# Window attention with a Mish FFN: weight pieces taken apart in pairs, on VectorE and ACT alone

## The chip, the cores and the metric

The kernel runs on one core of a Trainium2 chip. The metric is the device time of one execution in microseconds (us); a kernel is measured by the median of several runs. In the profile PE is TensorE (PEld its weight loads), DVE is VectorE, ACT is ScalarE, POOL is GpSimd, and SP is the engine whose queue issues the DMAs.

## The reference, cut to what matters

```python
def _attn_ref(q, k, v):            # q, k, v: 8 x 8 x 576 x 64
    scores = np.matmul(q, k.transpose(0, 1, 3, 2)) / np.sqrt(D)
    scores = np.where((rel >= 0) & (rel < 64), scores, -1000000000.0)
    attn = np.exp(scores - np.max(scores, axis=-1, keepdims=True))
    attn = attn / (np.sum(attn, axis=-1, keepdims=True) + 1e-09)
    return np.matmul(attn, v)

def _moe_ref(x, w_in, w_out):      # x: 4608 x 512, w_in: 512 x 2048, w_out: 2048 x 512
    h = x @ w_in
    sp = np.where(h > 20.0, h, np.log1p(np.exp(np.minimum(h, 20.0))))
    return ((h * np.tanh(sp)) @ w_out)
```

The two weight matrices are float64. The rest is float32.

## The kernel before, in words

The 4608 tokens go through in twelve chunks of 384. A chunk has an attention part (four pairs of heads) and then an FFN part of sixteen steps, one for each block of 128 hidden features. One step's FFN-in is twelve matmuls of 384 columns into `h_ps` (line 195): every product is made of three, high by high, high by low and low by high, since activations and weights are both held as a rounded high part and a rest. VectorE takes the minimum `t` (line 202), ACT applies four functions (lines 203, 208, 209, 210), VectorE multiplies (line 212), and ACT or POOL makes the high part `gh` and POOL the rest `gl` (line 217). FFN-out is nine matmuls of 512 columns into three accumulators (line 230) and follows two steps behind. `h_ps` has two buffers.

The weights come as 64-bit words and are taken apart on the core, in the program's first part, while chunk 0's attention and its first FFN steps run. `load_w` (line 242) handles one piece of 512 columns: a DMA of 512 KB into `st` (three buffers, line 245), the absolute value on ACT (line 251), a clamp (line 252), three bit operations on VectorE (lines 254 to 256) that build the float32 value `wa`, a rounded copy on ACT (line 257: `wi_h` or `wo_h`) and a subtraction (line 258: `wi_l` or `wo_l`). For a piece of the first matrix POOL clamps and VectorE subtracts; for one of the second VectorE clamps and POOL subtracts. So there are 32 pieces, and VectorE has 128 weight operations of 512 columns: 32 of each of lines 254, 255 and 256, 16 of line 252 and 16 of line 258.

Seven pieces are asked for among chunk 0's attention and two at each of its FFN steps (`take_w`). Eight steps of chunk 0 run alone, then they alternate with chunk 1's. Within that the order of each engine's instructions is set by the framework's scheduler, not by the order of the source. All loads are issued by SP, in one queue.

The program's first two chunks and the third transpose the probabilities on PE and copy them to `pT`, one half on ACT and one on VectorE (line 172).

Of the kernel before, what the change touches and what calls it, by code (L numbers as in the profile page):

```python
# [20 lines left out]
BIG = float(np.array(0x47EFFFFF, np.uint32).view(np.float32))  # L21
WP = 512


@with_exitstack
def tile_window_attn_mish_ffn(
# [45 lines left out]
    for j in range(2):  # L72
        m = const.tile([P, P], F32, name=f"mask{j}")
# [4 lines left out]
    wi_h = const.tile([P, NF, NC_, P], F32R, name="wi_h")
    wi_l = const.tile([P, NF, NC_, P], F32R, name="wi_l")
    wo_h = const.tile([P, NF, DO], F32R, name="wo_h")  # L80
    wo_l = const.tile([P, NF, DO], F32R, name="wo_l")
# [72 lines left out]
    def att_transpose(c, p, pr):  # L154
        pT = next(pTs)
        if c > 2:


            tr = ap_.tile([P, P // 32, HM, 32], F32, name="tr", tag="pr", bufs=2)
            nc.vector.transpose(tr.rearrange("p k j i -> p j k i"),  # L160
                                pr.rearrange("p j (k i) -> p j k i", i=32))
            for r in range(0, P, 32):
                for k in range(0, P, 32):
                    if 0 <= k - r % BLK <= BLK:
                        nc.sync.dma_start(pT[k:k + 32, r // 32, :, :], tr[r:r + 32, k // 32, :, :])
            return pT
        for h in range(2):
            t_ps = (bank(c, p, "t_ps") if c else ps_h.tile([P, CH], F32, name="t_ps", tag="h_ps")
                    ).rearrange("p (m k) -> p m k", k=P)
            for m in range(NM):  # L170
                nc.tensor.transpose(t_ps[:, m, :], pr[:, h * NM + m, :], ident)  # L171
            (nc.scalar.copy if h == 0 else nc.vector.tensor_copy)(
                pT[:, :, h * NM:(h + 1) * NM, :].rearrange("p r m i -> p m r i"),
                t_ps.rearrange("p m (r i) -> p m r i", i=32))
        return pT
# [13 lines left out]
    def ffn_in(c, x, f, alone=False):  # L189
        xh, xl = x  # L190
        h_ps = ps_h.tile([P, CH], F32, name="h_ps", tag="h_ps")
        n = 0
        for cc in range(NC_):
            for w, xx in ((wi_h, xh), (wi_h, xl), (wi_l, xh)):
                nc.tensor.matmul(h_ps, w[:, f, cc, :], xx[:, cc, :], start=n == 0, stop=n == 3 * NC_ - 1)  # L195
# [64 lines left out]
    def load_w_in(f):  # L260
        load_w(w_in[f].rearrange("p c f -> p (c f)"), wi_h[:, f, :, :].rearrange("p c f -> p (c f)"),
               wi_l[:, f, :, :].rearrange("p c f -> p (c f)"), True)

    def load_w_out(f):
        load_w(w_out[f], wo_h[:, f, :], wo_l[:, f, :], False)


    class Att:
# [17 lines left out]
        def transpose(self, p):  # L286
            self.pT[p] = att_transpose(self.c, p, self.pr.pop(p))
# [36 lines left out]
    todo_w = [(load_w_in, 0)]  # L324
    for f in range(NF):
        todo_w += [(load_w_in, f + 1)] * (f + 1 < NF) + [(load_w_out, f)]

    def take_w(n):
        for _ in range(min(n, len(todo_w))):
            w, f = todo_w.pop(0)  # L330
            w(f)

# [83 lines left out]
```

## Time and profile before

| What | us |
|---|---|
| Median of 3 runs (993.81 to 995.67) | 994.03 |
| The profiled execution | 995.3 |
| Its span, first to last instruction | 993.5 |
| PE busy | 946.5 (95%) |
| VectorE busy | 491.8 (50%) |
| ACT busy | 631.4 (64%) |
| POOL busy | 328.8 (33%) |

The profile shows one execution. Busy shares are averages over the span: the first 120 us look different from the rest. Matmuls are pipelined, and a busy PE is not PE at its peak. The granted clock of TensorE has two levels, 1.2 and 2.4 GHz; 1.00 means 2.4 GHz throughout a stretch.

### The profile page before, as it was taken

Reading aid. Unit: us, or ns where it says so; the run is one execution under the profiler, and the core shown is the slowest. Engines: PE = TensorE matmul, PEld = TensorE weight load, DVE = VectorE, ACT = ScalarE, POOL = GpSimd, SP = SyncE. Lnnn points to the kernel's source line nnn. Section 1 sums busy time; section 2 is a strip of 40 time slices with the busy share of each in tenths; the row PEclk is TensorE's granted clock in tenths of the full one; section 3 lists DMA queues with packets and bytes.
Section 4 is the critical chain, followed back from the end, with each engine's and each line's share of the span. In section 5 each row is a group of like instructions: output and inputs, shape, how many; then the busy total and the mean of one; then the engine's idle time right before and its main releaser. Section 6 shows DMA issues by size and latency. Waiting matters only on the chain.

```text
span 993.5 us, 18088 instructions
## 1 busy us (share of the span) xinstructions
PE 946.5 (95%) x6408; PEld 821.4 (83%) x6408; DVE 491.8 (50%) x1352; ACT 631.4 (64%) x1525; POOL 328.8 (33%) x419
## 2 busy tenths in 40 slices
PE   4696699998999999999999999999999999999998
PEld 3585599886888888888888888888888888888996
DVE  6799874444444454444454453453443543543222
ACT  5667676664666666665665666666665665666664
POOL 2243463321333333323333323323333333333333
PEclk8787899997999999999999999999999999999999
DMA  7565420123221221331221221221231221310000
GB/s 240 188 194 161 143 85 1 49 68 111 66 69 54 89 69 42 88 83 42 88 83 43 89 81 45 86 83 46 84 80 47 85 74 43 97 39 13 32 1 32
DMA packets 82649, 77.34 MB, mean 78 GB/s; under 512 B 10368, under 2 KB 73856, under 8 KB 82560
## 3 DMA queue, kind: packets, MB, share of 16 engines
q1 hardware_dynamic: 82560, 76.19, 25.5%
q8 instruction: 51, 0.84, 0.4%
q14 instruction: 38, 0.31, 0.1%
HBM read 56.10 MB, written 9.44 MB: 66 GB/s over the span
## 4 chain that ended last, share of the span: by engine, by line
PE 87%; DVE 6%; DMA 2%; ACT 2%; issue 1%; SPq 0%; ACTq 0%; POOL 0%; DVEq 0%; POOLq 0%
PE h_ps L195 40%; PE acc L230 38%; PE s_ps L128 4%; PE o_ps L184 4%; DMA st<-w_out 2%; DVE wa L256 1%; DVE wa L255 1%; DMA st<-w_in 1%; ACT pr L141 1%; PE t_ps L171 1%; DVE wa L252 0%; DVE wi_l L258 0%; DVE wa L254 0%; DVE t L212 0%; ACT wa L251 0%
## 5 line engine op out<-in xcount | busy, mean ns | idle before, releaser
L195 PE MATMUL h_ps<-xh,wi_h 128*128 128x384 f32 x768 | 267.8, 349 | 13.6 <-DVE t L212 12.3
L216 POOL TENSOR_SCALAR gh<-t 128x384 fp32r<-128x384 f32 x176 | 90.7, 515 | 550.1 <-DVE t L212 504.0
L195 PE MATMUL h_ps<-xh,wi_l 128*128 128x384 f32 x768 | 263.7, 343 | 0.0
L195 PE MATMUL h_ps<-xl,wi_h 128*128 128x384 f32 x768 | 263.3, 343 | 0.0
L203 ACT ACTIVATE t<-t 128x384 f32<-128x384 f32 x192 | 100.5, 524 | 237.2 <-DVE t L202 237.2
L230 PE MATMUL acc<-wo_l,gh 128*128 128x512 f32 x576 | 227.0, 394 | 0.0
L230 PE MATMUL acc<-wo_h,gh 128*128 128x512 f32 x576 | 226.4, 393 | 0.5 <-POOL gh L216 0.5
L212 DVE SCALAR_TENSOR_TENSOR t<-t,h_ps 128x384 f32<-128x384 f32 x176 | 96.9, 550 | 250.3 <-ACT t L210 249.9
L217 POOL TENSOR_TENSOR gl<-t,gh 128x384 fp32r<-128x384 f32 x192 | 197.2, 1027 | 32.8 <-ACT gh L214 18.2
L230 PE MATMUL acc<-wo_h,gl 128*128 128x512 f32 x576 | 206.8, 394 | 0.0
L195 PEld LDWEIGHTS h_ps<-xh,wi_h 128*128 128x128 f32 x768 | 147.0, 192 | 28.5 <-DVE t L212 14.6
L195 PEld LDWEIGHTS h_ps<-xl,wi_h 128*128 128x128 f32 x768 | 147.4, 192 | 8.1 <-issue 1.9
L195 PEld LDWEIGHTS h_ps<-xh,wi_l 128*128 128x128 f32 x768 | 147.5, 192 | 1.1 <-issue 0.2
L202 DVE TENSOR_SCALAR t<-h_ps 128x384 f32<-128x384 f32 x192 | 106.6, 556 | 63.2 <-PE h_ps L195 55.8
L141 ACT ACTIVATE pr<-pr,mx 128x128 f32<-128x128 f32 x288 | 111.8, 390 | 38.0 <-DVE mx L138 38.0
L230 PEld LDWEIGHTS acc<-wo_h,gl 128*128 128x128 f32 x576 | 107.4, 188 | 23.7 <-issue 1.5
L230 PEld LDWEIGHTS acc<-wo_h,gh 128*128 128x128 f32 x576 | 109.1, 189 | 17.6 <-POOL gh L216 0.9
L230 PEld LDWEIGHTS acc<-wo_l,gh 128*128 128x128 f32 x576 | 108.9, 189 | 16.6
L209 ACT ACTIVATE t<-t,half_b 128x384 f32<-128x384 f32 x192 | 118.2, 616 | 5.4
L208 ACT ACTIVATE t<-t,one_b 128x384 f32<-128x384 f32 x192 | 118.1, 616 | 5.1
L210 ACT ACTIVATE t<-t 128x384 f32<-128x384 f32 x192 | 100.4, 524 | 5.6
L138 DVE CUSTOM_DVE_ANT_0 pr<-s_ps,mask 128x128 f32<-128x128 f32 x288 | 65.3, 286 | 60.7 <-PE s_ps L128 60.7
(49 smaller groups left out, 693.3 us busy)
## 6 DMA issues: line engine op xcount, KB each, us to landing
v_t<-vN SPq DMA_DIRECT2D x48, 384.0 KB, 3.6
k_t<-kT SPq DMA_DIRECT2D x47, 224.0 KB, 3.0
pT<-tr SPq DMA_DIRECT2D x432, 24.0 KB, 1.8
out<-o SPq DMA_DIRECT2D x36, 256.0 KB, 2.3
q_t<-qT SPq DMA_DIRECT2D x47, 192.0 KB, 2.5
st<-w_in SPq DMA_DIRECT2D x16, 512.0 KB, 4.4
st<-w_out SPq DMA_DIRECT2D x16, 512.0 KB, 3.4
q_t<-qT SPq DMA_DIRECT2D x3, 64.0 KB, 2.1
```

The costliest lines, as they stand in the source:

```text
L138: nc.vector.tensor_tensor_reduce(out=pr[:, j, :], in0=s_ps[h][:, m, :], in1=mk, op0=ALU.add, op1=ALU.min, scale=-0.125, scalar=3.0e38, acc ...
L141: nc.scalar.activation(pr[:, j, :], pr[:, j, :], AF.Exp, bias=mx[:, j:j + 1], scale=-1.0, accum_out=sm[:, j:j + 1])
L195: nc.tensor.matmul(h_ps, w[:, f, cc, :], xx[:, cc, :], start=n == 0, stop=n == 3 * NC_ - 1)
L202: nc.vector.tensor_scalar(t, h_ps, 20.0, None, ALU.min)
L203: nc.scalar.activation(t, t, AF.Exp)
L208: nc.scalar.activation(t, t, AF.Square, bias=one_b)
L209: nc.scalar.activation(t, t, AF.Ln, bias=half_b, scale=0.5)
L210: nc.scalar.activation(t, t, AF.Exp, scale=-1.0)
L212: nc.vector.scalar_tensor_tensor(t, t, -1.0, h, ALU.add, ALU.mult)
L216: nc.gpsimd.tensor_scalar(gh, t, 1.0, 0.0, ALU.mult, ALU.add)
L217: nc.gpsimd.tensor_tensor(gl, t, gh.bitcast(F32), ALU.subtract)
L230: nc.tensor.matmul(acc[t], a[:, ts_], w[:, f, :], start=f == 0 and i == 0, stop=f == NF - 1 and i == 2)
```

## The change

The host lays both pieces of a step side by side, 1024 columns, in one array `w`. `load_w` (now line 245) loads them with one DMA of 1 MB and takes them apart together: one ACT operation for the absolute value, five VectorE operations (clamp, line 258; three bit operations, 260 to 262; subtraction, 267), one rounded copy on ACT. POOL has no part in it. A piece is loaded into memory of its own, which later holds the step's high and low parts; from the fourth on, a load waits for the last bit operation of the third piece before it. VectorE has 80 weight operations of 1024 columns: 32 with one tensor as input (lines 258 and 260) and 48 with two. Four pieces are asked for among chunk 0's attention and one at each FFN step of chunk 0. Chunk 1's second half of `pT` is copied by ACT too.

```diff
-        st = mp.tile([P, WP], I64, name="st", bufs=3, tag="st")
-        nc.sync.dma_start(st, src)
+        st = const.tile([P, 2 * WP], I64, name="st", tag=f"w{f}")
+        dma = nc.sync.dma_start(st, w[f])
+        if f >= 3:
+            tc.add_manual_dep(dma.ins, used[f - 3].ins.name, SYNC, reason="pace")
...
-        a = mp.tile([P, WP], U32, name="wa", tag="t", bufs=4)
+        a = mp.tile([P, 2 * WP], U32, name="wa", bufs=2)
         af = a.bitcast(F32)
         nc.scalar.activation(af, hi.bitcast(F32), AF.Abs)
-        (nc.gpsimd if first else nc.vector).tensor_scalar(af, af, BIG, TINY, ALU.min, ALU.max)
+        nc.vector.tensor_scalar(af, af, BIG, TINY, ALU.min, ALU.max)
...
+        ws.append(const.tile([P, 2, 2, WP], F32R, name="w", tag=f"w{f}"))
+        wh, wl = ws[f][:, :, 0, :], ws[f][:, :, 1, :]
         nc.scalar.copy(wh, af)
-        (nc.vector if first else nc.gpsimd).tensor_tensor(wl, af, wh.bitcast(F32), ALU.subtract)
+        nc.vector.tensor_tensor(wl, af, wh.bitcast(F32), ALU.subtract)
...
-            (nc.scalar.copy if h == 0 else nc.vector.tensor_copy)(
+            (nc.scalar.copy if h == 0 or c == 1 else nc.vector.tensor_copy)(
...
-            take_w(2)
+            take_w()
```

The scheduler makes another order of it. On VectorE, this is the place of the tenth and eleventh step's `t` (the row with x2; line 202 before, 203 now), ahead of it and behind. Before:

```order
L252 TENSOR_SCALAR wa<-wa 128x512
L254 TENSOR_SCALAR wa<-wa 128x512 x2
L255 SCALAR_TENSOR_TENSOR wa<-st,wa 128x512 x2
L256 SCALAR_TENSOR_TENSOR wa<-st,wa 128x512 x2
L202 TENSOR_SCALAR t<-h_ps 128x384 x2
L258 TENSOR_TENSOR wi_l<-wa,wi_h 128x512
L252 TENSOR_SCALAR wa<-wa 128x512
L254 TENSOR_SCALAR wa<-wa 128x512 x2
L255 SCALAR_TENSOR_TENSOR wa<-st,wa 128x512
L212 SCALAR_TENSOR_TENSOR t<-t,h_ps 128x384
L255 SCALAR_TENSOR_TENSOR wa<-st,wa 128x512
L212 SCALAR_TENSOR_TENSOR t<-t,h_ps 128x384
```

The same place in the change:

```order
L267 TENSOR_TENSOR w<-wa,w 128x2x512
L261 SCALAR_TENSOR_TENSOR wa<-st,wa 128x1024
L262 SCALAR_TENSOR_TENSOR wa<-st,wa 128x1024
L187 TENSOR_TENSOR xl_577<-o_ps,xh_576 128x384
L267 TENSOR_TENSOR w<-wa,w 128x2x512
L203 TENSOR_SCALAR t<-h_ps 128x384 x2
L213 SCALAR_TENSOR_TENSOR t<-t,h_ps 128x384 x2
L203 TENSOR_SCALAR t<-h_ps 128x384
L213 SCALAR_TENSOR_TENSOR t<-t,h_ps 128x384
```

The first row with x2 of `t` has 99 of the 128 weight operations ahead of it before, and all 80 of the 80 in the change; nothing of the weights stands behind it.

On SP, the loads from the first weight piece on. Before:

```order
L245 DMA st<-w_in 128x512
L105 DMA q_t<-qT 128x384
L107 DMA k_t<-kT 128x448
L114 DMA v_t<-vN 128x6x128
L245 DMA st<-w_in 128x512
L114 DMA v_t<-vN 128x6x128
L105 DMA q_t<-qT 128x384
L107 DMA k_t<-kT 128x448
L245 DMA st<-w_out 128x512
```

The same place in the change:

```order
L248 DMA st<-w 128x1024
L105 DMA q_t<-qT 128x384
L107 DMA k_t<-kT 128x448
L114 DMA v_t<-vN 128x6x128 x2
L248 DMA st<-w 128x1024
L105 DMA q_t<-qT 128x384
L107 DMA k_t<-kT 128x448
L248 DMA st<-w 128x1024
```

The places of the weights' loads are nearly the same; each carries twice the bytes.

## Rows read from the trace of the kernel before

**Rows 1.** Windows: length, busy us of PE, PEld, DVE, ACT, POOL; PEclk, DMA, GB/s.

```profile
6.00:50.00 44.00, 26.64 (x272) 20.41 (x274) 36.50 (x133) 28.38 (x93) 8.21 (x8) 0.80 0.69 223
50.00:117.40 67.40, 57.54 (x355) 49.56 (x351) 64.64 (x134) 47.39 (x113) 29.82 (x25) 0.85 0.54 168
117.40:123.80 6.40, 0.11 (x1) 0.00 (x0) 4.38 (x10) 5.68 (x12) 1.89 (x2) 0.82 0.45 164
123.80:128.30 4.50, 4.48 (x14) 4.38 (x15) 3.81 (x6) 1.75 (x3) 4.29 (x4) 0.50 0.37 116
128.30:230.00 101.70, 101.70 (x641) 89.68 (x640) 51.18 (x129) 68.49 (x157) 36.27 (x42) 1.00 0.16 50
```

**Rows 2.** Chain of waits, 110 to 140 us: start, length, what.

```profile
115.04 1.29 DVE wa L255 x2
...
123.22 0.56 DVE t L212
...
123.82 4.21 PE h_ps L195 x12
...
134.43 2.08 PE h_ps L195 x12
```

**Rows 3.** Groups on VectorE, 0 to 117.40 us: busy, mean ns, idle ahead.

```profile
L256 DVE SCALAR_TENSOR_TENSOR wa<-st,wa 128x512 uint32<-128x512 uint32 x25 | 23.4, 939 | 0.0
L255 DVE SCALAR_TENSOR_TENSOR wa<-st,wa 128x512 uint32<-128x512 uint32 x25 | 19.6, 795 | 0.1
L254 DVE TENSOR_SCALAR wa<-wa 128x512 uint32<-128x512 uint32 x25 | 11.3, 464 | 0.4 <-POOL wa L252 0.2
L138 DVE CUSTOM_DVE_ANT_0 pr<-s_ps,mask 128x128 f32<-128x128 f32 x48 | 11.0, 283 | 9.4 <-PE s_ps L128 9.4
L258 DVE TENSOR_TENSOR wi_l<-wa,wi_h 128x512 fp32r<-128x512 f32 x12 | 10.3, 858 | 0.2 <-ACT wi_h L257 0.2
L252 DVE TENSOR_SCALAR wa<-wa 128x512 f32<-128x512 f32 x12 | 5.6, 464 | 3.7 <-ACT wa L251 3.6
L202 DVE TENSOR_SCALAR t<-h_ps 128x384 f32<-128x384 f32 x9 | 4.9, 548 | 0.7 <-PE h_ps L195 0.7
...
L172 DVE COPY pT<-t_ps 128x384 f32<-128x384 f32 x8 | 4.4, 545 | 0.0
...
L145 DVE TENSOR_SCALAR sm<-sm 128x3 f32<-128x3 f32 x8 | 1.5, 191 | 1.5 <-ACT pr L141 1.5
```

**Rows 4.** Groups on VectorE, 160 to 230 us: a 768-column operation.

```profile
L151 DVE TENSOR_TENSOR pr<-pr,sm 128x768 f32<-128x768 f32 x4 | 3.8, 954 | 0.1
```

**Rows 5.** Tile `wa`: shortest, median and longest duration in ns.

```profile
L254 DVE TENSOR_SCALAR wa<-wa x32: 410/420/1528, 10.4 to 151.1; 128x512 uint32<-128x512 uint32 x32
...
L256 DVE SCALAR_TENSOR_TENSOR wa<-st,wa x32: 674/686/1753, 12.7 to 153.1; 128x512 uint32<-128x512 uint32 x32
```

**Rows 6.** Timeline, POOL at 98 us, then VectorE: start, length, operation.

```profile
98.08 1.33 POOL L258 TENSOR_TENSOR wo_l<-wa,wo_h 128x512 fp32r<-128x512 f32 x1 [4.55 <-ACT wo_h L257]
...
54.92 0.95 DVE L252 TENSOR_SCALAR wa<-wa 128x512 f32<-128x512 f32 x1 [0.99 <-ACT wa L251]
...
98.21 1.75 DVE L256 SCALAR_TENSOR_TENSOR wa<-st,wa 128x512 uint32<-128x512 uint32 x1
...
112.67 1.32 DVE L258 TENSOR_TENSOR wi_l<-wa,wi_h 128x512 fp32r<-128x512 f32 x1 [0.22 <-ACT wi_h L257]
...
117.45 1.02 DVE L202 TENSOR_SCALAR t<-h_ps 128x384 f32<-128x384 f32 x2
```

**Rows 7.** Windows, 10 to 20 us, when the first loads land.

```profile
10.00:20.00 10.00, 5.60 (x69) 4.08 (x62) 9.02 (x39) 6.21 (x22) 1.12 (x2) 0.83 0.92 320
```

**Rows 8.** Waits of SP's DMA queue, 0 to 120 us: total, times, longest.

```profile
SPq L245 <- DVE wa L256: 78.2, 22, 7.4
```

**Rows 9.** Timeline of ACT at the restart, 116 to 131 us.

```profile
121.35 1.10 ACT L209 ACTIVATE t<-t,half_b 128x384 f32<-128x384 f32 x2
122.36 0.92 ACT L210 ACTIVATE t<-t 128x384 f32<-128x384 f32 x2
```

More of the change, by code (lines that the diff above doesn't have):

```diff
@@ L21 @@
 BIG = float(np.array(0x47EFFFFF, np.uint32).view(np.float32))
+SYNC = mybir.DependencyInfo(mybir.DependencyClass.Sync, mybir.DependencyReason.DATA)
 WP = 512
@@ L31, in tile_window_attn_mish_ffn @@
     vN: bass.AP,
-    w_in: bass.AP,
-    w_out: bass.AP,
+    w: bass.AP,
     out: bass.AP,
@@ L38, in tile_window_attn_mish_ffn @@
     NPAIR, _, NT = qT.shape
-    NF, _, NC_, _ = w_in.shape
-    DO = w_out.shape[2]
+    NF = w.shape[0]
+    DO = out.shape[1]
+    NC_ = NPAIR
     CH = 384
@@ L76, in tile_window_attn_mish_ffn @@
         firsts.append(m)
[L78 to L81, printed above, removed]
+    ws = []
     pTs = [const.tile([P, P // 32, HM, 32], F32, name=f"pT{i}") for i in range(2)]
@@ L193, in ffn_in @@
         for cc in range(NC_):
-            for w, xx in ((wi_h, xh), (wi_h, xl), (wi_l, xh)):
-                nc.tensor.matmul(h_ps, w[:, f, cc, :], xx[:, cc, :], start=n == 0, stop=n == 3 * NC_ - 1)
+            for part, xx in ((0, xh), (0, xl), (1, xh)):
+                nc.tensor.matmul(h_ps, ws[f][:, 0, part, cc * P:(cc + 1) * P], xx[:, cc, :],
+                                 start=n == 0, stop=n == 3 * NC_ - 1)
                 n += 1
@@ L228, in ffn_out @@
             ts_ = slice(t * P, (t + 1) * P)
-            for i, (a, w) in enumerate(((gh, wo_h), (gh, wo_l), (gl, wo_h))):
-                nc.tensor.matmul(acc[t], a[:, ts_], w[:, f, :],
+            for i, (a, part) in enumerate(((gh, 0), (gh, 1), (gl, 0))):
+                nc.tensor.matmul(acc[t], a[:, ts_], ws[f][:, 1, part, :],
                                  start=f == 0 and i == 0, stop=f == NF - 1 and i == 2)
@@ L234, in ffn_store @@
         for t in range(NTT):
-            o = mp.tile([P, DO], F32, name="o", bufs=3, tag="st")
+            o = mp.tile([P, DO], F32, name="o", bufs=3)
             if t % 2 == 0:
@@ L240, in ffn_store, with load_w @@
             nc.sync.dma_start(out[c * CH + t * P:c * CH + (t + 1) * P, :], o)
-    def load_w(src, wh, wl, first):
-        st = mp.tile([P, WP], I64, name="st", bufs=3, tag="st")
-        nc.sync.dma_start(st, src)
+    used = []
+    def load_w(f):
+        st = const.tile([P, 2 * WP], I64, name="st", tag=f"w{f}")
+        dma = nc.sync.dma_start(st, w[f])
+        if f >= 3:
+            tc.add_manual_dep(dma.ins, used[f - 3].ins.name, SYNC, reason="pace")
         words = st.bitcast(U32).rearrange("p (n two) -> p n two", two=2)
         lo, hi = words[:, :, 0], words[:, :, 1]
-        a = mp.tile([P, WP], U32, name="wa", tag="t", bufs=4)
+        a = mp.tile([P, 2 * WP], U32, name="wa", bufs=2)
         af = a.bitcast(F32)
         nc.scalar.activation(af, hi.bitcast(F32), AF.Abs)
-        (nc.gpsimd if first else nc.vector).tensor_scalar(af, af, BIG, TINY, ALU.min, ALU.max)
+        nc.vector.tensor_scalar(af, af, BIG, TINY, ALU.min, ALU.max)
         nc.vector.tensor_scalar(a, a, 3, 0x3FFFFFFF, ALU.logical_shift_left, ALU.bitwise_and)
         nc.vector.scalar_tensor_tensor(a, hi, 0xC0000000, a, ALU.bitwise_and, ALU.bitwise_or)
-        nc.vector.scalar_tensor_tensor(a, lo, 29, a, ALU.logical_shift_right, ALU.bitwise_or)
+        used.append(nc.vector.scalar_tensor_tensor(a, lo, 29, a, ALU.logical_shift_right, ALU.bitwise_or))
+        af = af.rearrange("p (m n) -> p m n", n=WP)
+        ws.append(const.tile([P, 2, 2, WP], F32R, name="w", tag=f"w{f}"))
+        wh, wl = ws[f][:, :, 0, :], ws[f][:, :, 1, :]
         nc.scalar.copy(wh, af)
-        (nc.vector if first else nc.gpsimd).tensor_tensor(wl, af, wh.bitcast(F32), ALU.subtract)
[L260 to L265, printed above, removed]
+        nc.vector.tensor_tensor(wl, af, wh.bitcast(F32), ALU.subtract)
     class Att:
@@ L321, in flush, with take_w @@
             ffn_store(c, accs.pop(c))
[L324 to L331, printed above, removed]
+    todo_w = list(range(NF))
+    def take_w():
+        if todo_w:
+            load_w(todo_w.pop(0))
     HEAD = 8
@@ L348, in tile_window_attn_mish_ffn @@
     atts[0].load(0, "qk")
-    take_w(1)
+    take_w()
     atts[0].load(1, "qk")
     atts[0].load(0, "v")
-    take_w(1)
     atts[0].load(1, "v")
@@ L358, in tile_window_attn_mish_ffn @@
         fn(p)
-        if at == p:
-            take_w(1)
-    take_w(1)
+        if at == p and p != 1:
+            take_w()
     atts[1].plan(0, 2 * HEAD / (NPAIR + 1))
@@ L377, in tile_window_attn_mish_ffn @@
         if c == 0:
-            take_w(2)
+            take_w()
     while pend:
@@ L399 @@
     w_in, w_out = np.asarray(inputs["moe_w_in"]), np.asarray(inputs["moe_w_out"])
-    w_in = np.ascontiguousarray(w_in.reshape(w_in.shape[0] // P, P, -1, P).transpose(2, 1, 0, 3))
+    w_in = w_in.reshape(w_in.shape[0] // P, P, -1, P).transpose(2, 1, 0, 3)
+    w = np.concatenate([w_in.reshape(w_in.shape[0], P, -1), w_out.reshape(-1, P, w_out.shape[1])], 2)
     arrays = {
@@ L405 @@
         "vN": led(np.ascontiguousarray(v.reshape(B, NP_, 2, S, D).transpose(1, 0, 3, 2, 4)).reshape(NP_, B * S, 2 * D), 1),
-        "w_in": w_in.view(np.int64),
-        "w_out": np.ascontiguousarray(w_out).reshape(-1, P, w_out.shape[1]).view(np.int64),
+        "w": w.view(np.int64),
     }
```

## The prediction

> **What bounds the kernel now.** I read the busy time by stretch first, then the chain of waits, then the groups of instructions on VectorE. From 128.30 us to 230 PE is busy in all 101.70 us at a granted clock of 1.00 [rows 1]: there it is the bound, and what VectorE, ACT, POOL or the loads gain is worth nothing. Ahead of that, from 6 to 117.40, VectorE is busy 36.50 of 44.00 and 64.64 of 67.40 us, while PE has gaps and ends in one: 0.11 us busy between 117.40 and 123.80. So the weights' work lies in a stage that VectorE sets. The chain shows the hand-over: VectorE's `t` of line 212 at 123.22 releases the twelfth FFN-in step's matmuls at 123.82 [rows 2], and from there PE doesn't stop until the third chunk's attention. There the two orders on PE stand within one step's nine FFN-out matmuls of each other, and from the fourteenth step on they have the same work behind them. So the question is one: **by how much does the start of the twelfth step move?** All behind it is the same PE work.
>
> The mark I use is the pair of line 202 operations (tenth and eleventh step) that VectorE begins at 117.45; the twelfth step follows 6.37 us later.
>
> **What stands ahead of the mark.** Before, 99 of the 128 weight operations: 25 each of lines 254, 255, 256, 12 of 258 and 12 of 252. Their busy time is 19.6 + 23.4 + 11.3 + 10.3 + 5.6 = 70.2 us [rows 3]. In the changed order all 80 stand ahead of it. The 29 operations that now run after the mark, beneath a PE that has no gap, lose that cover: this is the price of the change. The rest of VectorE's work ahead of the mark is the same but for the `pT` copies.
>
> **Price of the new operations.** Of the 80, 48 read two tensors (lines 261, 262, 267). None of 1024 columns is in the trace. 768 columns took 0.954 us [rows 4], 512 took 0.686 [rows 5]: 0.268 for 256 columns. One more such step gives 1.222 us, and 48 of them 58.7. The other 32 have one tensor (lines 258, 260). 512 columns took 0.420 [rows 5], three columns 0.191 [rows 3], so 512 columns more add about 0.23: 0.65 each, 20.8 in all. The ends for one are 0.42 (columns free) and 0.84 (nothing shared), which is -7.4 and +6.1 over the 32; I take 0.65 because the small row shows a fixed share. Sum 79.5 us.
>
> **Stalls.** In the 70.2 us there is waiting. At their medians the 99 would take 37 x 0.420 + 62 x 0.686 = 58.1, so 12.1 us are stretched operations. The operation of line 256 at 98.21 took 1.75 us, with a POOL subtraction begun 0.13 us ahead of it [rows 6]. Seventeen of the 99 are over 0.3 us longer than their median; ten began while POOL ran weight work and seven, from 54.92 to 112.67 [rows 6], while it ran the FFN's own subtraction (line 217). Those seven hold 5.1 us. POOL loses its weight work, so the ten go; the seven can stay. Ends 0 and 5.1; I take the middle, 2.6, since VectorE starts fewer operations and is nearly always running when POOL comes. The Trainium skill, SBUF — State Buffer, section Who interferes with whom, calls it an exclusive lock that whichever of the two starts first holds for its whole instruction. The row agrees; by that rule alone the term is anything up to the same 5.1.
>
> Changed weights less the old: 79.5 + 2.6 - 70.2 = **+11.9**. Neighbours overlap a little: two of line 255 took 1.29 together [rows 2], not 1.37. There are 19 fewer of these overlaps, 0.08 each: **+1.5**.
>
> **The copies.** Four `pT` copies of chunk 1 leave VectorE: 4 x (0.545 - 0.08) = **-1.9** [rows 3]. On ACT even their whole VectorE price, 2.2 us, has cover: ACT is busy 47.39 of 67.40 us [rows 1]. Without that cover they would be +2.2. ACT's own weight work keeps its columns and issues half the instructions; I cost it at nothing under the same cover.
>
> **Waits on VectorE.** After the first scores it was idle some 9.9 us ahead of the mark: 3.6 for ACT's absolute value, whose data were not loaded, 0.7 for line 195, 9.4 less the 6.2 of the program's start for scores, 1.5 for sums, the rest in bits [rows 3]. Loads are three whole pieces ahead now, so I credit 3.6. The 3.2 for scores and the 0.7 fell where VectorE had no loaded weights to take apart; now it has, so I credit both: -7.5. Against it the first two loads are twice as large and the first operations come late: 512 KB more each at the 320 GB/s of that stretch [rows 7] is 1.6 each, +3.3. Together **-4.2**. Ends: -9.9 if no wait is left, +3.3 if none goes.
>
> **The pacing wait.** The fourth load and later ones wait on SP for line 262 of three pieces before, and chunk 1's q, k and v loads stand behind them. Such a wait was there before too (78.2 us on SP, 22 times, for line 256 [rows 8]). I cost the exchange at nothing while loads run ahead of VectorE; without that cover one late 1 MB load costs 3.3. Bytes are equal.
>
> So the mark moves by 11.9 + 1.5 - 1.9 - 4.2 = +7.3.
>
> **From the mark to the twelfth step.** Before: 6.37 us (117.45 to 123.82) [rows 2, 6], with five weight operations between `t` and line 212. Now none stands there. What is left is `t` (0.55), ACT's four functions on two steps in pairs, up to the first result 0.92 + 1.10 + 1.10 + 0.46 = 3.6 (the square taken as the logarithm, the first exponential as the last) [rows 9], and line 212 (0.56): 4.7. **-1.7**. The twelfth step's matmuls ran at a granted clock of 0.50, that is 1.2 GHz, after the gap, and took 4.21 us instead of 2.08 [rows 1, 2]. PE has its gap in the new order too, so I leave that; at full clock it would be -2.1.
>
> Sum **+5.6 us**. The profiled execution took 995.3 us around a span of 993.5, so it would become 1000.9. It lies 1.3 above the median of the three runs, 994.0; against that the forecast is **999.6 us**. A run of this kernel can be told from no change by about 0.2%, 2 us.
>
> **The rivals.**
> *VectorE waits for nothing (faster).* Place: VectorE ahead of the mark. If POOL never holds it up and every wait but the start's goes, the first loads' included, the sum is 79.5 - 70.2 + 1.5 - 1.9 - 9.9 - 1.7 = -2.7, with PE at full clock -4.8: 989 to 991 us. It decides from the point where stalls, waits and late first loads, 2.6 + 2.4 + 3.3 = 8.3 in my sum, fall under 0.7 (2.8 at full clock). For it: 12.1 us of stalls and 9.9 of waits are in the rows. Against it: line 217 still comes once a step, and the first 1 MB can't land as 512 KB did. The Trainium skill, Perfetto Trace Analysis, section Optimizing Scalar/DVE Operations, has rules on both sides: larger operations help a saturated engine, and a saturated VectorE may hand work to GpSimd, though their shared port may spoil it. The trace bears out the first within an operation (0.954 for 768 columns, not 1.5 times 0.686) and the shared port. Chance 0.11.
>
> *The gains meet the price (no change).* About half of those 8.3 us don't come, or PE keeps 2.4 GHz through its restart: +5.6 less 4 or so, 994 to 996 us. Chance 0.14.
>
> *POOL starves (slower still).* Each `gl` of line 217 now waits behind 1.22 us operations instead of 0.69. PE takes its matmuls in order, so a late `gl` holds the next step. If each of the nine steps loses one such operation, 9 x 1.22 = 11 us more: 1011. Against it: FFN-out follows FFN-in by two steps, more than VectorE's longest operation. Chance 0.05.
>
> **How the numbers follow.** The forecast has 0.70, POOL's rival 0.05: slower 0.75. No change 0.14, faster 0.11. Its own ends don't fall together: stalls 2.6 to either side, waits 5.7 less or 7.5 more, the one-tensor price 7.4 and 6.1. The range is 994.0 to 1006.0, the forecast -5.6 and +6.4: it takes in most of the no-change case and leaves out the faster one and POOL's, under 0.2 together.
>
> **What would show it.** Right: in the changed profile VectorE's two-tensor operations of 1024 columns at about 1.22 us and the one-tensor ones at 0.65; the last weight operation near 125 us instead of 155; VectorE without idle time from 25 to 120; the pair of line 203 near 125 and the twelfth step's matmuls some 4.7 us behind it, near 130; the stretch after that unchanged in length. Wrong: the twelfth step before 124; operations of 1024 columns far from these prices; PE idle later than 135 us for other reasons than the third chunk's scores.

## The result and the profile after

| | Median us | Range | Ratio to before, 95% interval |
|---|---|---|---|
| Before, 4 runs | 994.11 | 993.81 to 995.67 | |
| Changed, 4 runs | 1002.85 | 1001.97 to 1003.87 | 1.0085 [1.0068, 1.0103] |

Slower by some 8.5 us, where 5.6 were forecast. The profiled execution of the changed kernel took 1001.97 us around a span of 1000.2; the span is 6.7 us longer than before.

Windows of the changed kernel; columns as in [rows 1]: length, busy us of PE, PEld, DVE, ACT, POOL, then PEclk, DMA share, GB/s.

```profile
6.00:50.00 44.00, 25.41 (x244) 18.72 (x244) 41.89 (x120) 27.81 (x80) 0.00 (x0) 0.98 0.82 288
50.00:121.40 71.40, 58.34 (x385) 48.52 (x385) 70.57 (x123) 55.63 (x114) 15.31 (x9) 0.88 0.48 166
121.40:126.05 4.65, 0.00 (x1) 0.01 (x1) 1.63 (x5) 3.83 (x8) 0.00 (x0) 0.50 0.00 0
126.05:130.60 4.55, 4.55 (x14) 4.55 (x15) 0.64 (x2) 0.51 (x1) 2.48 (x3) 0.51 0.00 0
130.60:230.00 99.40, 99.40 (x616) 87.81 (x617) 35.08 (x104) 61.90 (x140) 29.07 (x36) 1.00 0.10 30
```

The picture is the one of [rows 1]: a stage that VectorE sets, a gap of PE, a restart at 1.2 GHz (0.51), then PE without a pause. VectorE now fills its stage: 70.57 of 71.40 us.

Chain of waits of the changed kernel, 110 to 140 us: start, length, what.

```profile
120.26 0.04 DVE w L267
...
121.40 0.56 DVE t L203
...
125.44 0.56 DVE t L213
...
126.05 5.77 PE h_ps L195 x20
...
136.63 2.11 PE h_ps L195 x12
```

The mark, the pair of `t`, starts at 121.40 in the place of 117.45 (+3.95); the twelfth step at 126.05 in the place of 123.82 (+2.2). So 4.5 us of the 6.7 are not here at all. They are in the steady stretch: a step's matmuls take 2.11 us where [rows 2] has 2.08.

Groups on VectorE in the changed kernel, 0 to 121.30 us: busy us, mean ns, idle ahead of them.

```profile
L261 DVE SCALAR_TENSOR_TENSOR wa<-st,wa 128x1024 uint32<-128x1024 uint32 x16 | 20.2, 1265 | 0.0
L267 DVE TENSOR_TENSOR w<-wa,w 128x1024 fp32r<-128x1024 f32 x16 | 20.2, 1260 | 0.7 <-ACT w L266 0.7
L262 DVE SCALAR_TENSOR_TENSOR wa<-st,wa 128x1024 uint32<-128x1024 uint32 x16 | 19.4, 1214 | 0.0
L258 DVE TENSOR_SCALAR wa<-wa 128x1024 f32<-128x1024 f32 x16 | 12.3, 771 | 0.1
L260 DVE TENSOR_SCALAR wa<-wa 128x1024 uint32<-128x1024 uint32 x16 | 12.2, 764 | 0.1
L138 DVE CUSTOM_DVE_ANT_0 pr<-s_ps,mask 128x128 f32<-128x128 f32 x48 | 10.9, 282 | 7.4 <-PE s_ps L128 7.4
L203 DVE TENSOR_SCALAR t<-h_ps 128x384 f32<-128x384 f32 x9 | 4.9, 543 | 0.1
...
L172 DVE COPY pT<-t_ps 128x384 f32<-128x384 f32 x4 | 2.2, 548 | 0.0
L145 DVE TENSOR_SCALAR sm<-sm 128x3 f32<-128x3 f32 x8 | 1.2, 159 | 0.5 <-ACT pr L141 0.5
```

Tile `wa` in the changed kernel: shortest, median and longest duration in ns.

```profile
L258 DVE TENSOR_SCALAR wa<-wa x16: 675/683/1509, 11.2 to 112.6; 128x1024 f32<-128x1024 f32 x16
L261 DVE SCALAR_TENSOR_TENSOR wa<-st,wa x16: 1192/1216/2033, 12.6 to 116.6; 128x1024 uint32<-128x1024 uint32 x16
```

### The profile page after: what moved, and what is told of

Read it like the earlier page. It is cut to its first block, busy times and chain, and to the rows that moved or that the text cites. A ratio compares the mean times of both kernels' runs of the same rounds, so it can differ in the third digit from the quotient of the medians.

```text
span 1000.2 us, 17919 instructions
## 1 busy us (share of the span) xinstructions
PE 949.7 (95%) x6408; PEld 822.5 (82%) x6408; DVE 482.5 (48%) x1300; ACT 631.1 (63%) x1497; POOL 295.3 (30%) x387
## 4 chain that ended last, share of the span: by engine, by line
PE 86%; DVE 10%; ACT 2%; issue 1%; DMA 0%; SPq 0%; ACTq 0%; POOL 0%; DVEq 0%; POOLq 0%
PE h_ps L195 40%; PE acc L231 38%; PE s_ps L128 4%; PE o_ps L184 4%; DVE wa L261 2%; DVE wa L262 2%; DVE w L267 2%; DVE wa L258 1%; DVE pr L138 1%; DVE wa L260 1%; DVE t L213 1%; DVE t L203 1%; ACT pr L141 0%; DVE pr L151 0%; DMA k_t<-kT 0%
## 5 line engine op out<-in xcount | busy, mean ns | idle before, releaser
L195 PE MATMUL h_ps<-xh,w 128*128 128x384 f32 x1536 | 440.0, 346 | 18.0 <-DVE t L213 14.0
L231 PE MATMUL acc<-w,gh 128*128 128x512 f32 x1152 | 343.3, 395 | 0.5 <-POOL gh L217 0.5
L195 PEld LDWEIGHTS h_ps<-xh,w 128*128 128x128 f32 x1536 | 285.4, 191 | 34.3 <-DVE t L213 15.5
L195 PE MATMUL h_ps<-xl,w 128*128 128x384 f32 x768 | 262.9, 342 | 1.5 <-DVE xl L187 1.5
L231 PEld LDWEIGHTS acc<-w,gh 128*128 128x128 f32 x1152 | 214.3, 188 | 33.3 <-POOL gh L217 0.9
L231 PE MATMUL acc<-w,gl 128*128 128x512 f32 x576 | 208.1, 394 | 0.0
L195 PEld LDWEIGHTS h_ps<-xl,w 128*128 128x128 f32 x768 | 146.8, 191 | 10.1 <-DVE xl L187 2.6
L231 PEld LDWEIGHTS acc<-w,gl 128*128 128x128 f32 x576 | 107.5, 188 | 24.7 <-issue 1.5
L184 PE MATMUL o_ps<-pT,v_t 128*64 128x64 f32 x1152 | 57.4, 237 | 6.4 <-DVE pT L172 5.0
L128 PE MATMUL s_ps<-k_t,q_t 64*64 64x128 f32 x1152 | 58.1, 298 | 5.1 <-DMA k_t<-kT 5.1
```

Source lines behind the costliest of these rows:

```text
L128: nc.tensor.matmul(s_ps[h][par * BLK:(par + 1) * BLK, m, :], q_t[rows, n * BLK:(n + 1) * BLK], k_t[rows, n * BLK:n * BLK + P], start=True, ...
L184: nc.tensor.matmul(o_ps[rows, n * BLK:(n + 1) * BLK], v_t[:, n, rows], pT[:, 2 * par:2 * par + 2, h * NM + m, :], start=True, stop=True)
L195: nc.tensor.matmul(h_ps, ws[f][:, 0, part, cc * P:(cc + 1) * P], xx[:, cc, :], start=n == 0, stop=n == 3 * NC_ - 1)
L231: nc.tensor.matmul(acc[t], a[:, ts_], ws[f][:, 1, part, :], start=f == 0 and i == 0, stop=f == NF - 1 and i == 2)
```

## The experiments

Twelve kernels ran, each with runs of the kernel before on the same chip. The last five columns are from each profiled execution: the start of the first matmul of the n-th FFN-in step, less the same in the kernel before (123.82 us for the twelfth). What a run gains or loses up to the twelfth step, to the twentieth, at the third chunk's attention (32 to 40) and in the steady rest can be read off a line.

| Run | Median us | Ratio [interval] | 12th | 20th | 32nd | 40th | 192nd |
|---|---|---|---|---|---|---|---|
| changed | 1002.85 | 1.0085 [1.0068, 1.0103] | +2.2 | +2.2 | +2.5 | +2.6 | +6.7 |
| e1_weights_by_step | 993.61 | 0.9997 [0.9985, 1.0009] | -0.9 | -0.9 | -0.9 | -2.4 | -2.4 |
| e2_t_places | 1002.76 | 1.0084 [1.0069, 1.0098] | +1.1 | +0.5 | +0.9 | +0.5 | +4.8 |
| e3_paced | 1000.58 | 1.0062 [1.0047, 1.0076] | -5.1 | -2.0 | -1.6 | -0.3 | +4.2 |
| e4_pool_back | 1008.18 | 1.0146 [1.0127, 1.0165] | +8.7 | +8.5 | +8.8 | +8.8 | +12.9 |
| e5_w_down_64 | 997.15 | 1.0037 [1.0025, 1.0048] | +3.3 | +2.7 | +2.7 | +2.7 | +2.7 |
| e6_w_up_64 | 997.91 | 1.0051 [1.0039, 1.0062] | -2.0 | -1.7 | -1.4 | -1.4 | +2.6 |
| e7_held_and_down_64 | 992.15 | 0.9988 [0.9978, 0.9998] | -4.5 | -3.1 | -2.4 | -3.6 | -3.6 |
| e8_halves | 999.93 | 1.0067 [1.0054, 1.0080] | +0.9 | -1.1 | -0.8 | +0.2 | +4.8 |
| e9_halves_held_six | 991.49 | 0.9974 [0.9963, 0.9985] | -7.8 | -3.6 | -2.5 | -3.7 | -3.7 |
| e10_halves_down_64 | 996.48 | 1.0033 [1.0020, 1.0046] | +0.3 | -2.0 | -2.0 | -0.1 | +1.0 |
| e11_whole_held_six | 996.54 | 1.0030 [1.0020, 1.0040] | -5.3 | -3.9 | -2.6 | -1.3 | -0.2 |
| e12_x_up_64 | 996.50 | 1.0030 [1.0020, 1.0040] | +1.4 | +2.0 | +0.8 | +0.8 | +0.8 |

One profiled execution places the twelfth step only within a spread of some 2 us: e1 and e6 have the order of the kernel before and reach it 0.9 and 2.0 us sooner; the changed kernel, e5 and e12 have one order too and lie at +2.2, +3.3 and +1.4. The means of the three executions of each order are 3.3 us apart.

### Where does the drift come from?

From the fortieth step to the last, the changed kernel loses 4.1 us, some 27 ns a step on average. The order on PE is the same in that stretch, and so are its waits. Only addresses differ. From the start of one FFN-in matmul to the start of the next, averaged over steps 33 to 190 (without the few spacings over 200 ns), the difference lies mostly at positions 3 to 6 of the twelve: together 689 ns before and 714 in the changed kernel.

**e1_weights_by_step** lays the old kernel's weights out as the new one's.

```diff
-    wi_h = const.tile([P, NF, NC_, P], F32R, name="wi_h")
...
+    ws = [const.tile([P, 2, 2, WP], F32R, name=f"w{f}") for f in range(NF)]
```

> The kernel before with one edit: the weights lie by step, 8 KB for each (in high, in low, out high, out low, 2 KB apart), as in the changed kernel, in the place of four arrays of 32 KB. Every engine's order, every operation's size and every other buffer stay. In the changed kernel the steps behind the twelfth run 4.2 us longer over the whole execution, and the FFN-in's matmuls at positions 3 to 6 of 12 follow each other at 177, 182, 176 and 180 ns in the place of 173, 170, 171 and 175. Theory 'places of the weights': the drift comes here too, all else stays: twelfth step near 123.8 us, the four positions together near 714 ns in the place of 689, 998.3 us, ratio 1.004 to the kernel before. Theory 'places of t, gh and gl': nothing changes, ratio 1.000, 689 ns. Theory 'something else' (fetching of the program, the number of instructions): 1.000 as well.

**e2_t_places** gives the new kernel the old addresses of the FFN's buffers.

```diff
+    op = ctx.enter_context(tc.tile_pool(name="op", bufs=2))
...
-        t = mp.tile([P, CH], F32, name="t", tag="t", bufs=4)
+        t = mp.tile([P, WP], F32, name="t", tag="t", bufs=4)[:, :CH]
...
-            o = mp.tile([P, DO], F32, name="o", bufs=3)
+            o = op.tile([P, DO], F32, name="o", bufs=2)
```

> The changed kernel with t, gh and gl at the byte addresses that they have in the kernel before (t 2 KB apart in the place of 1.5; the output's buffer o is two deep in the place of three to make room). The weights stay as in the changed kernel. Theory 'places of t, gh and gl': the drift goes: the FFN-in's positions 3 to 6 back at 689 ns together, 1002.9 - 4.2 = 998.7 us, ratio 1.004 to the kernel before. Theory 'places of the weights': the drift stays, 714 ns, 1002.9 us, ratio 1.0085. The twelfth step near 126 us in both. The smaller o costs nothing where PE has work to go on with; if a store does hold the next, it shows at the ends of chunks, not in the FFN-in's spacing.

Both theories fell: e1 stays at 689 ns and 0.9997, e2 at 716 ns and 1.0084. What the drifting kernels had in common was smaller than a buffer. In the changed kernel two constants of 32 bytes come ahead of the weights, which then begin at byte 24768, 64 past a multiple of 128; before, and in e1, at 18560, a multiple.

**e5_w_down_64** and **e6_w_up_64** are mirror images; no engine's order changes.

```diff
-    half_b = const.tile([P, 1], F32, name="half_b")
+    half_b = xp.tile([P, 1], F32, name="half_b")
...
-    one_b = const.tile([P, 1], F32, name="one_b")
+    one_b = xp.tile([P, 1], F32, name="one_b")
```

```diff
+    half_b, one_b = (const.tile([P, 1], F32, name=n) for n in ("half_b", "one_b"))
     wi_h = const.tile([P, NF, NC_, P], F32R, name="wi_h")
```

> The changed kernel with its weights 64 bytes lower in SBUF: two constants of one column (half_b, one_b) lie behind the weights in the place of ahead of them, so the first weight begins at byte 24704, a multiple of 128, in the place of 24768, which is 64 past one. Before, the weights began at 18560, a multiple of 128; in the run that laid the old kernel's weights out by step (no drift) they did too; in the run with moved t, gh and gl (drift) they didn't. Every order and every other address stays. Theory 'the 64 bytes': the drift behind the twelfth step goes: FFN-in's matmuls at positions 3 to 6 at 689 ns together in the place of 714, 1002.9 - 4.2 = 998.7 us, ratio 1.004 to 1.005. Rival 'something in the program' (fewer instructions, their fetching): 714 ns and 1.0085.

> The mirror of the run with the weights 64 bytes lower: the kernel before with the same two constants ahead of its four weight arrays, so that these begin 64 bytes higher, at 18624. Every order stays; beside the weights only pT lies 64 bytes higher. Theory 'the 64 bytes': the kernel before gets the drift: twelfth step near 123.8 us, then 26 ns more for each step, positions 3 to 6 near 714 ns, 994.1 + 4.2 = 998.3 us, ratio 1.004. Rival 'something in the program': 1.000 and 689 ns.

**e12_x_up_64** asks whether the weights' own place counts, or their distance from what they are multiplied with.

```diff
+    nc.gpsimd.memset(xp.tile([P, 16], F32, name="pad"), 0.0)
     one_b = const.tile([P, 1], F32, name="one_b")
```

> The changed kernel with 64 unused bytes behind the weights: the weights stay at 24768, 64 past a multiple of 128, and x, t, gh, gl and all other buffers behind them move up by 64. So the FFN-in's two inputs lie as far apart within 128 bytes as they did before (there the weights at a multiple of 128 and xh at 155840, 64 past one; here the other way round; in the changed kernel both are 64 past). Theory 'a place of its own' (weights must begin at a multiple of 128): the drift stays, FFN-in 2.11 us and FFN-out 2.06 in the chain, ratio 1.0085. Theory 'the distance' (what counts is where the two inputs of a matmul lie against each other): the drift goes, 2.08 and 2.05 us, 998.7 us, ratio 1.004 to 1.005.

One FFN-out and one FFN-in step from the chain of waits, 600 to 700 us. The kernel before:

```profile
609.13 2.05 PE acc L230 x9
611.18 2.08 PE h_ps L195 x12
```

The changed kernel:

```profile
613.71 2.06 PE acc L231 x9
615.77 2.11 PE h_ps L195 x12
```

e5, its weights 64 bytes lower:

```profile
611.86 2.05 PE acc L231 x9
613.91 2.08 PE h_ps L195 x12
```

e6, the kernel before with its weights 64 bytes higher:

```profile
609.65 2.06 PE acc L229 x9
611.71 2.11 PE h_ps L196 x12
```

e12, weights as in the changed kernel, all buffers behind them 64 bytes higher:

```profile
609.90 2.05 PE acc L232 x9
611.95 2.08 PE h_ps L195 x12
```

The 64 bytes take the drift away (e5: flat at +2.7 from the twentieth step on) and make it (e6: -1.4 to +2.6). A third pair agrees: e8 and e10, below, have one order, and the 64 bytes are worth 3.4 us between them. In e12 the weights are still 64 past a multiple of 128, and the drift is gone. So the weights' own place doesn't decide; it counts together with the place of the buffers behind them. Whether the two must differ, or one of them must be at a multiple of 128, isn't shown: no run has weights and x both at one. By the ratios the drift is 8.5 us less 3.7 (e5) or 3.0 (e12), and 5.1 [3.9, 6.2] in e6 alone: about 5 us. Without it the change costs 3.0 to 3.7 us, not 8.5.

### What does the head pay for?

**e3_paced** holds the last four pieces back at their loads; **e7_held_and_down_64** at ACT's first operation, with the weights moved as in e5.

```diff
+        if f >= 12:
+            tc.add_manual_dep(dma.ins, tops[2 * f - 14].ins.name, SYNC, reason="late")
+        elif f >= 3:
...
-        nc.vector.tensor_scalar(t, h_ps, 20.0, None, ALU.min)
+        tops.append(nc.vector.tensor_scalar(t, h_ps, 20.0, None, ALU.min))
...
-        if c == 0:
+        while todo_w and (todo_w[0] < 12 and c == 0 or 2 * todo_w[0] - 14 <= n):
             take_w()
```

e7 has the last two of these edits too, those of e5, and in the place of the first one:

```diff
-        nc.scalar.activation(af, hi.bitcast(F32), AF.Abs)
+        ab = nc.scalar.activation(af, hi.bitcast(F32), AF.Abs)
+        if f >= 12:
+            tc.add_manual_dep(ab.ins, tops[2 * f - 14].ins.name, SYNC, reason="late")
```

> The changed kernel with its last four weight pieces (20 of the 80 VectorE operations) held back: their loads wait for the exponential's input t of the 11th, 13th, 15th and 17th FFN-in step. Nothing else is edited. Theory of the prediction (the price is weight work that stands ahead of the mark and has lost PE's cover): those 20 take 4 x (2 x 0.684 + 3 x 1.215) = 20 us off VectorE ahead of the mark. PE has 17.7 us of idle time between 50 and 126 us to give back, so the gain is less than that: the twelfth step 6 to 15 us earlier than 126.05, and 988 to 997 us, ratio 0.993 to 1.003, with the drift still in it. Rival 'loads, not operations': the start is held by the 1 MB loads or by ACT's share, and holding pieces back gains nothing: the twelfth step within 1 us of 126, ratio 1.0085. Rival 'late pieces': the held pieces come too late and PE stops for them behind the twelfth step: idle time of PE between 130 and 200 us, ratio over 1.0085.

> The changed kernel with the weights 64 bytes lower and with its last four pieces held back, but not at their loads as in the paced run, where the loads then stood in the chain of waits at 115, 129 and 147 us for 4.7 to 5.3 us each: the loads come as early as in the changed kernel, and ACT's absolute value of the piece waits for t of the 11th, 13th, 15th and 17th step. Theory of the prediction with 'the 64 bytes': twelfth step near 118.7 as in the paced run, no piece late behind it, no drift: 1000.6 - 4.2 and up to 3 for the late loads, 993 to 996.5 us, ratio 0.999 to 1.0025. Rival 'the gain is given back whatever comes late': twelfth step near 118.7, PE idle for 3 us or more between 126 and 200 again, and ratio 1.002 to 1.004 where the drift goes, 1.006 where it doesn't.

Windows about the twelfth step, and from there to 200 us. The changed kernel:

```profile
117.40:126.00 8.60, 1.78 (x25) 1.06 (x21) 4.84 (x8) 5.36 (x10) 0.00 (x0) 0.67 0.15 46
126.00:200.00 74.00, 73.95 (x392) 67.08 (x393) 22.47 (x56) 44.76 (x92) 23.91 (x29) 0.97 0.05 17
```

e3:

```profile
117.40:126.00 8.60, 7.33 (x27) 7.07 (x28) 5.91 (x7) 3.72 (x8) 2.63 (x3) 0.64 0.21 88
126.00:200.00 74.00, 71.98 (x388) 63.29 (x387) 39.32 (x73) 52.28 (x101) 24.29 (x27) 1.00 0.17 60
```

e7:

```profile
126.00:200.00 74.00, 72.62 (x402) 64.12 (x400) 38.86 (x72) 50.37 (x100) 24.45 (x28) 1.00 0.05 17
```

The chain of waits of e3, 90 to 260 us, holds two of the late loads:

```profile
128.76 4.77 DMA st<-w
...
146.57 5.27 DMA st<-w
```

In e3 the twelfth step comes 7.4 us sooner than in the changed kernel, as the theory had it, but 3.1 are given back by the twentieth, where loads are late (PE idle 2.02 us after 126), and the drift is still there. So its median, 1000.58, lies above the forecast's 988 to 997. e7 loads early (only the last piece, at 120.5 us, later than in the changed kernel), gives back 2.1 from the twelfth step to the 32nd (VectorE and ACT now have weight work there) and doesn't drift. Its 992.15 is a little better than forecast: 0.9988 against e5's 1.0037. Holding four of sixteen pieces is worth 4.9 us. That shows the prediction's mechanism, the lost cover, with the drift out of the way; the scheduler's order changes with the held pieces, so the 4.9 holds that too.

**e4_pool_back** gives POOL its share again.

```diff
-        nc.vector.tensor_scalar(af, af, BIG, TINY, ALU.min, ALU.max)
+        for e, s in ((nc.gpsimd, slice(0, WP)), (nc.vector, slice(WP, 2 * WP))): e.tensor_scalar(af[:, s], af[:, s], BIG, TINY, ALU.min, ALU.max)
...
-        nc.vector.tensor_tensor(wl, af, wh.bitcast(F32), ALU.subtract)
+        for i, e in enumerate((nc.vector, nc.gpsimd)): e.tensor_tensor(wl[:, i], af[:, i], wh[:, i].bitcast(F32), ALU.subtract)
```

> The changed kernel with POOL's old share back: POOL takes the clamp of the in-half and the subtraction of the out-half of each piece, 512 columns each; loads and the other operations stay joined at 1024. Theory of the prediction: VectorE gives up 16 x (0.684 - 0.42) + 16 x (1.215 - 0.686) = 12.7 us ahead of the mark, and gets back some of the 7 us that it lost to POOL's weight work before: the mark 3 to 10 us earlier than 121.4, the time 993 to 1000 us, ratio 0.999 to 1.006, with the drift still in it. Rival 'POOL's lock costs what it takes off': VectorE's operations beside POOL's stretch by as much as the share is worth, the mark within 2 us of 121.4, ratio 1.007 to 1.010. Rival 'waits come back': VectorE waits for POOL's clamp at the head of each chain, idle time of VectorE ahead of the mark over 5 us more than the changed kernel's.

Timelines of e4, POOL first, then VectorE: start, length, operation.

```profile
64.18 1.47 POOL L267 TENSOR_TENSOR w<-wa,w 128x512 fp32r<-128x512 f32 x1 [4.25 <-ACT w L266]
...
68.49 1.28 POOL L267 TENSOR_TENSOR w<-wa,w 128x512 fp32r<-128x512 f32 x1 [0.37 <-ACT w L266]
```

```profile
64.44 1.76 DVE L267 TENSOR_TENSOR w<-wa,w 128x512 fp32r<-128x512 f32 x1
...
68.62 1.43 DVE L258 TENSOR_SCALAR wa<-wa 128x512 f32<-128x512 f32 x1
...
127.80 1.02 DVE L203 TENSOR_SCALAR t<-h_ps 128x384 f32<-128x384 f32 x2 [0.32 <-PE h_ps L195]
```

VectorE's weight operations take 86.4 us in e4 (groups up to 130 us: 21.0 + 20.7 + 18.9 + 15.4 + 10.4) against 84.3, though 12.7 us of work went to POOL. An operation that starts behind POOL's is held: 1.76 and 1.43 us in the place of 0.69 and 0.42. The attention's operations of lines 145, 147 and 151 are held too: 13.6 us together ahead of the mark, 9.5 in the changed kernel. The mark is at 127.80, 6.4 later, so it is worse than the rival had it. The two halves of a subtraction wait for the same ACT operation here and can start together, as at 64.18 and 64.44; before the change a piece's subtraction was done by one of the two engines alone. So with the pieces joined, giving POOL its share back costs 5 to 6 us. What POOL's share was worth with the pieces apart, as it stood before the change, wasn't tried.

**e8_halves** cuts VectorE's operations in two; **e10_halves_down_64** is the same with the weights moved; **e9_halves_held_six** and **e11_whole_held_six** hold six pieces (`f >= 10`, `tops[2 * f - 12]`), with and without halves, weights moved. `halves` are the columns 0 to 511 and 512 to 1023.

```diff
-        nc.vector.tensor_scalar(af, af, BIG, TINY, ALU.min, ALU.max)
+        for s in halves: nc.vector.tensor_scalar(af[:, s], af[:, s], BIG, TINY, ALU.min, ALU.max)
...
-        nc.vector.tensor_tensor(wl, af, wh.bitcast(F32), ALU.subtract)
+        for i in range(2): nc.vector.tensor_tensor(wl[:, i], af[:, i], wh[:, i].bitcast(F32), ALU.subtract)
```

> The changed kernel with VectorE's 80 operations on the weights cut into 160 of 512 columns, each pair one behind the other; the loads, ACT's operations and VectorE's whole share stay. Theory of the prediction (an operation has a fixed share, 0.156 us by the medians here: 2 x 0.420 - 0.684 and 2 x 0.686 - 1.215): 80 x 0.156 = 12.5 us more on VectorE ahead of the mark, less what neighbours overlap, 80 x 0.08 = 6.4: the mark 6 to 12 us later than 121.4, 1009 to 1015 us, ratio 1.015 to 1.021. Rival 'the size gives nothing' (the starts lie beneath other work or overlap wholly): mark within 2 us, ratio 1.007 to 1.010.

> The run with VectorE's operations in halves, with the weights 64 bytes lower and nothing held back. By the 64 bytes alone its 999.9 us lose 4 us: 995.5 to 996.5, ratio 1.002 to 1.0035, the twelfth step at 124.8 as there. If the halves' gain was chance of one order and not of the grain, the twelfth step is back near 126 and the ratio at 1.004.

> VectorE's operations of 512 columns, the last six pieces held back (ACT's absolute value of each waits for t of the 9th, 11th, 13th, 15th, 17th and 19th step), weights 64 bytes lower; loads and engines' shares as in the changed kernel. The halves alone gave 2.8 us against the changed kernel, holding four pieces and the 64 bytes 10.7. Theory 'they add' (smaller operations let t and line 213 in earlier, holding takes weight work off VectorE ahead of the mark): 992.2 - 2.8, and up to 3 more from the two further pieces: 986 to 990 us, ratio 0.993 to 0.997, the twelfth step near 116. Rival 'one gap, closed once': both close the same gap of PE, 991 to 993 us, ratio 0.998 to 1.000. Rival 'late pieces': PE idle over 3 us between 126 and 200, ratio over 1.000.

> Operations of 1024 columns with the last six pieces held back in the place of four, weights 64 bytes lower. Theory 'they add' of the run with halves: ten more operations off VectorE ahead of the mark, but the grain stays coarse: 990 to 992.5 us, ratio 0.997 to 0.9995, twelfth step 117 to 121. Rival 'late pieces': the held pieces come too late, PE stops behind the twelfth step, 993 us or more, ratio over 1.000. With the run of halves it tells what the size of the operation is worth when the order is not held back by the number of pieces.

Groups on VectorE of e8, 0 to 140 us:

```profile
L262 DVE SCALAR_TENSOR_TENSOR wa<-st,wa 128x512 uint32<-128x512 uint32 x32 | 22.9, 731 | 0.0
...
L259 DVE TENSOR_SCALAR wa<-wa 128x512 f32<-128x512 f32 x32 | 12.1, 417 | 0.1
```

Its timeline on VectorE before the twelfth step:

```profile
118.53 0.54 DVE L203 TENSOR_SCALAR t<-h_ps 128x384 f32<-128x384 f32 x1
...
122.14 0.54 DVE L203 TENSOR_SCALAR t<-h_ps 128x384 f32<-128x384 f32 x1
...
125.22 0.54 DVE L213 SCALAR_TENSOR_TENSOR t<-t,h_ps 128x384 f32<-128x384 f32 x1
```

And its window:

```profile
117.40:126.00 8.60, 6.63 (x32) 5.28 (x32) 8.36 (x17) 7.65 (x12) 4.85 (x3) 1.00 0.00 0
```

Both expectations missed e8. Its weight operations do take longer, 92.8 us against 84.3 (all five groups up to 140 us; neighbours' overlap gives part of it back), yet it isn't slower, and at the 32nd step it is 3.3 us ahead of the changed kernel (-0.8 against +2.5). The scheduler made another order of the smaller operations: the tenth and eleventh `t` come one at a time (118.53, 122.14), and PE works 6.63 of the 8.60 us in the place of 1.78. Its granted clock stays at 1.00 there, that is 2.4 GHz, and the twelfth step takes 2.35 us; at 1.2 GHz it took 4.21 before the change [rows 2]. e10, with the same order, stands at -2.0 at the 32nd step, where e5 and e12 have +2.7 and +2.0. The size of an operation set the order, not only the price. The Trainium skill, Perfetto Trace Analysis, section Optimizing Scalar/DVE Operations, says to group operations where the engine is saturated and to break them up where it isn't but makes gaps elsewhere. VectorE is saturated here (17.40 of the 17.40 us ahead of that window), and breaking up closed most of the gap all the same.

By ratios e8's gain is small (1.0067 against 1.0085, the intervals overlap), and e10, at 996.48 as its first expectation had it, is no faster than e5. The two of them carry something else: in e3, e8, e10 and e11 PE's order from the third chunk's attention on is another than in the rest. From the 32nd step to the fortieth these four lose 1.0 to 1.9 us; the others gain up to 1.5 or lose 0.1. PE's one long wait there, for line 213, takes 4.7 to 5.4 us in these four and 3.3 to 3.6 in the ten others. On PE's timeline, first e11, then e7:

```profile
241.04 0.69 PE L195 MATMUL h_ps<-xh,w 128*128 128x384 f32 x1 [5.40 <-DVE t L213]
```

```profile
239.52 0.69 PE L195 MATMUL h_ps<-xh,w 128*128 128x384 f32 x1 [3.64 <-DVE t L213]
```

Of those four, e10 and e11 have no drift by address, and still lose 1.1 from the fortieth step to the end. With that order go 3.0 us in e10 and 2.4 in e11; no run changed the order alone.

In e9 the twelfth step came where it was forecast (116.05), and 5.3 us of it were gone by the 32nd: with six pieces late, VectorE and ACT are in PE's way (PE idle 3.00 us from 126 to 200, two of the late pieces in the chain of waits at 143 and 155, and behind the first of them one FFN-in and one FFN-out at 2.97 and 3.03 us in the place of 2.08 and 2.05, at a granted clock of 0.72). At the 32nd step it stands where e7 does, -2.5 against -2.4. So smaller operations and held pieces close the same gap once; e9 ends at 991.49, by its number that rival. e11 has the number of "late pieces", 996.5, but not their place: it stands at -2.6 at the 32nd step like e7 and e9, and loses the rest behind it, by that other order.

**e9 beats both kernels**: 0.9974 [0.9963, 0.9985], 2 to 3 us under the kernel before and some 11 under the changed one; e7, with four pieces and whole operations, 0.9988 [0.9978, 0.9998].

## Why the prediction was right, and where it wasn't

The sign and the range held, and the mechanism was there: the weight work without its cover (e7). But it made only 3.0 to 3.7 of the 8.5 us, and that the forecast of 5.6 came as near as it did is partly luck. Two errors of opposite sign met: the head was overpriced, and the stretch behind it, about 5 us, wasn't priced at all.

- **"All behind it is the same PE work"**, with its sign "the stretch after that unchanged in length", is the step that failed. The work is the same, but not its time: 27 ns more a step, about 5 us by the ratios, from 64 bytes of address (e5, e6, e12). The diff shows it only through the order in which buffers are allocated.
- **Price of the operations**: 1.215 us for two tensors (1.222 forecast), right. One tensor took 0.684, not 0.65: 1.1 us over the 32. The sum at medians is 32 x 0.684 + 48 x 1.215 = 80.2 (79.5).
- **Stalls**: the five groups took 84.3, so 4.1 (2.6), nearer to the end at which line 218's stalls stay: six operations are over 0.3 us longer than their median, by 4.1 us together, and each runs beside line 218 on POOL. Changed weights less the old: +14.1, not +11.9.
- **The copies**: 4.4 to 2.2 us, as forecast. PE waited 0.2 us for ACT's copies between 100 and 130.
- **Waits**: VectorE's idle time ahead of the mark fell from 16.0 to 8.7 us, -7.3 where -4.2 was put. The groups show it against [rows 3]: scores 9.4 to 7.4, absolute value 3.7 to 0.1, `t` 0.7 to 0.1, sums 1.5 to 0.5. The larger first loads cost 1.2, not 3.3: the first scores' operation came at 7.36 in the place of 6.16. This is what made the head cheaper than forecast. The faster rival (-9.9) was a little nearer on the waits and wrong on the stalls, of which it had none and 4.1 stayed.
- Other operations took 1.1 less, line 151 (4.4 to 3.8) and the sums of line 145 above all. With POOL's share back, in e4, they take 5.4 and 2.4. 14.1 - 2.2 - 7.3 - 1.1 = +3.5; the 0.45 left to 3.95 is overlap (1.5 put).
- **From the mark to the twelfth step**: 4.65 us (4.7), and that step at 1.2 GHz as before: right.
- The twelfth step at +2.2 in that execution, +5.6 forecast. The runs without drift give 3.0 to 3.7 by the ratios.
- **POOL starves** didn't come: PE's only long waits from 100 to 130 us were for line 213, 9.0 us.
- The way of reckoning, busy time ahead of a fixed pair, held for an order that stays. It failed for e8, where the order itself changed, and operations that took more time in all closed most of the gap.

## What to carry to other kernels

When a change moves buffers, compare one steady step before and after, to the hundredth of a microsecond: a few bytes of address can cost more than all the rest of the edit (here about 5 us against 3 to 4), and a shift by 64 bytes with no order changed tells it in one run. In a stage that one engine sets, work that isn't due belongs behind the work that a later engine waits for; larger operations are worth their saved share only if the urgent ones still get in between. Work given to a second engine can cost more than it takes off, where its operations hold up the first one's (1.76 us in the place of 0.69 in e4).

## What the runs showed of the hardware

Matmuls of one shape took another time by where their inputs lie. The first bytes within 128, weights / x / `gh`: 0 / 64 / 0 in the kernel before, e1 and e5: 2.08 and 2.05 us for FFN-in and FFN-out. 64 / 64 / 0 in the changed kernel, e2 and e6: 2.11 and 2.06. 64 / 0 / 64 in e12: 2.08 and 2.05. Most of it is in the FFN-in, at positions 3 to 6 of 12 (e5 689, e6 713, e12 689 ns).

No one rule of distance covers both kinds. The FFN-in was slow with weights and x both at 64; the FFN-out was slower by 0.01 us with weights and `gh` 64 apart, and had its 2.05 again with both at 64. e12 moved x, `gh` and all else behind the weights together, so which pair counts wasn't separated, and other places weren't tried.

What PE did just before counts too. In the changed kernel and in e6, of the steps 33 to 190 all 17 that follow straight on the scores' matmuls and all 8 that follow on the values' (line 184) have 693 to 696 ns at these positions, while 107 of the 120 that follow on an FFN-out have some 720. Attention work on the other engines isn't needed for it: the last chunk, which has none beside it, has its 720 as well. Why it is these positions stays open.

The Trainium skill, TensorE: Matmul & The Clock Gate, section Step-by-step: what each phase is for, states that loading the next weights takes no SBUF read bandwidth from the running matmul. These runs can't show what stands in a matmul's way; they show that its time depends on where the inputs lie.
